# Where the last gate piece and the split of the next group stand in a gated-linear-attention kernel followed by a multiplicative feed-forward block

## The chip, the cores and the metric

The kernel runs on one core of one Trainium2 chip. The metric is the device time of one execution in microseconds. The kernel before took 459.05 us, the median of three runs (457.19, 459.05, 459.93).

## What is computed

For each of 4 batches and 8 heads a recurrence runs over 768 time steps, with heads of 48 values; its output, laid out as 3072 tokens by 384 values, goes through a feed-forward block with two multiplied factors:

```python
for t in range(S):
    state = alpha[:, :, t, :, None] * state + np.einsum('bhd,bhe->bhde', k[:, :, t], v[:, :, t])
    y[:, :, t] = np.einsum('bhd,bhde->bhe', q[:, :, t], state)
...
a = x @ w1        # (3072, 384) @ (384, 1024)
b = x @ w2
h = a * b @ w3    # (1024, 1024)
return (h @ w_out).astype(np.float32)   # (1024, 384)
```

The weights come as 64-bit floats and are converted on the chip from their bits.

## The kernel before

**Part 1, the attention.** The sequence is cut into N = 24 chunks of 128 tokens, six to a batch. The loop over n (0 to 24) is a pipeline written out by hand. A step n does, in the order of the program:

- attend_state(n - 1) (L473; L483 in early steps): the state T times q of the chunk before, into two banks of PSUM.
- scores(n) (L431): the products of keys and queries of chunk n, with some of the products of chunk n - 1 between them (attend_low, L420). VectorE masks the result (ms, L441; L458 in early steps).
- transposed(n + 1) (L383): TensorE transposes the scaled queries and keys of the next chunk, ScalarE copies them to qkT (L385).
- attend(n - 1) (L496): the rest of the products of masked scores and values; ScalarE copies them to x (L493, L498), and SP stores x to HBM (xd).
- outer(n) (L395): the outer products of keys and values; VectorE adds them to the state (L405). Nothing at the last chunk of a batch (n = 5, 11, 17, 23).
- decayed(n + 2) (VectorE, L361) scales queries and keys of chunk n + 2 into qk; logs(n + 4) (ScalarE L326 and L330, VectorE L331) takes logarithms of alpha; decays(n + 3) (TensorE L348) sums them, and ScalarE takes exponentials e of the sums (L351, L352).

**The gates.** While attention goes on, the two factors of the feed-forward block are computed for chunks that are done, in five early groups: four of 3 chunks and one of 4. The group's input is loaded from xd (load_early: into part of the tile x3b, for the last group into free input tiles). Then split_early cuts it into a high, a low and a middle part in 32-bit floats of reduced form: ScalarE makes the high part (L536), VectorE the low (L537) and the middle one (L539), which lies partly in tile x and partly in x3b. There is one such pair of tiles, so a split writes over what the gates of the group before read.

A gate is one tile of 128 of the 1024 columns: two pieces, one for each factor, each of 9 matmuls (L569) into two banks, six for the first and three for the second. ScalarE moves the first bank out (L578), VectorE adds the second (L580). After the second piece VectorE multiplies the two factors (L617), and the tile before this one is stored on SP's queue (L643). The first four groups do four tiles each in part 1, thus eight pieces a group. They wait in the list fill; run(pieces) takes some of them, at three places of a step: behind outer, behind logs and its conversions, and at the step's end behind decays.

**Conversions of weights** go on between: convert(steps) takes the next stage of a weight block (ScalarE L246, L251, L262; VectorE L247 to L267).

**Order.** Within an engine the instructions need not run in the order of the program; tc.issue_after (through after_marks) puts the instructions of a block behind a marked one on its own engine. Engines wait for each other through semaphores. PSUM has eight banks, all from one pool (bank). SP issues the loads and, in part 1, the stores.

Groups begin at steps 6 (FIRST), 9, 13, 17 and 21: begin has the keys 3, 7, 11, 15 and 19, and a group begins at n = key + 2 (group 0 at 6).

**Behind part 1** come the late gates with 512 columns, the product of w3 and w_out (fold), and the projection of all 24 chunks (project).

## Time and profile before

| what | value |
|---|---|
| median of 3 runs | 459.05 us (457.19 to 459.93) |
| the profiled execution's own time | 456.97 us |
| its span, first to last instruction | 455.2 us |
| TensorE matmuls busy | 442.2 us, 97% |
| TensorE weight loads busy | 392.9 us, 86% |
| VectorE / ScalarE / GpSimd busy | 369.8 / 279.3 / 85.5 us |
| granted TensorE clock | 0.999 |
| part 1 | to about 182 us |

The steps are found by the pair of copies to qkT (L385) that each has. Between the copies of one step and of the next one the engines are busy as follows; the four stretches that begin with a split's step are 75.18, 103.90, 132.50 and 160.75 (the windows view: from and to, length, then PE, PEld, DVE, ACT busy in us):

| stretch | length | PE | PEld | DVE | ACT | pieces in it |
|---|---|---|---|---|---|---|
| 75.18 to 81.62 (n = 9) | 6.44 | 4.82 | 4.24 | 5.66 | 6.03 | 0 |
| 81.62 to 89.38 | 7.76 | 7.76 | 7.32 | 7.67 | 5.53 | 3 |
| 97.43 to 103.90 (n = 12) | 6.47 | 6.47 | 6.03 | 6.36 | 5.82 | 2 |
| 103.90 to 109.19 (n = 13) | 5.29 | 5.10 | 4.42 | 5.25 | 5.24 | 0 |
| 125.56 to 132.50 (n = 16) | 6.94 | 6.94 | 6.50 | 4.49 | 5.28 | 2 |
| 132.50 to 137.28 (n = 17) | 4.78 | 4.67 | 3.98 | 4.25 | 4.72 | 0 |
| 153.80 to 160.75 (n = 20) | 6.95 | 6.95 | 6.50 | 5.53 | 4.03 | 2 |
| 160.75 to 165.03 (n = 21) | 4.28 | 4.19 | 3.87 | 3.87 | 4.22 | 0 |

In rows of the timeline stand: start, duration, engine, line, operation, what is written and read, count, and in brackets the idle time before it with what ended it. A row can merge several instructions. In rows of waits: who waited for whom, us in total, times, longest.

### The profile page before, as it was taken

Reading aid. Unit: us, or ns where it says so; the run is one execution under the profiler, and the core shown is the slowest. Engines: PE = TensorE matmul, PEld = TensorE weight load, DVE = VectorE, ACT = ScalarE, POOL = GpSimd, SP = SyncE. Lnnn points to the kernel's source line nnn. Section 1 sums busy time; section 2 is a strip of 40 time slices with the busy share of each in tenths; the row PEclk is TensorE's granted clock in tenths of the full one; section 3 lists DMA queues with packets and bytes.
Section 4 is the critical chain, followed back from the end, with each engine's and each line's share of the span. In section 5 each row is a group of like instructions: output and inputs, shape, how many; then the busy total and the mean of one; then the engine's idle time right before and its main releaser. Section 6 shows DMA issues by size and latency. Waiting matters only on the chain.

```text
span 455.2 us, 11107 instructions
## 1 busy us (share of the span) xinstructions
PE 442.2 (97%) x4304; PEld 392.9 (86%) x4304; DVE 369.8 (81%) x600; ACT 279.3 (61%) x523; POOL 85.5 (19%) x171
## 2 busy tenths in 40 slices
PE   4999998999999999999999999999999999999996
PEld 2677797998988988888888888888888999999996
DVE  2799997999979898899998999999427576776671
ACT  4698966779688673978875766575436333333430
POOL 6244341335225330021121010100010000000000
PEclk9999999999999999999999999999999999999999
DMA  9999999999888763466775263600129555565411
GB/s 205 246 263 235 256 248 232 229 228 236 211 185 208 198 176 106 148 184 176 251 231 184 95 187 114 208 32 38 48 89 279 175 176 165 168 192 171 151 51 52
DMA packets 149381, 79.98 MB, mean 176 GB/s; under 512 B 97184, under 2 KB 138784, under 8 KB 149328
## 3 DMA queue, kind: packets, MB, share of 16 engines
q1 hardware_dynamic: 143840, 64.84, 53.4%
q0 software_dynamic: 5488, 14.43, 10.1%
q8 instruction: 34, 0.56, 0.5%
q14 instruction: 19, 0.16, 0.1%
HBM read 57.19 MB, written 22.06 MB: 174 GB/s over the span
## 4 chain that ended last, share of the span: by engine, by line
PE 94%; ACT 2%; DVE 1%; issue 1%; DMA 1%; DVEq 0%; ACTq 0%
PE bank L569 74%; PE bank L383 3%; PE bank L342 2%; PE bank L431 2%; PE bank L455 2%; PE bank L473 2%; PE bank L502 2%; PE bank L395 2%; PE bank L496 1%; PE bank L348 1%; PE bank L345 1%; PE bank L420 1%; PE bank L483 1%; DMA ac<-in_alpha_dram 1%; ACT x L536 0%
## 5 line engine op out<-in xcount | busy, mean ns | idle before, releaser
L569 PE MATMUL bank<-x,w 128*128 128x512 f32 (+1 forms) x688 | 161.8, 373 | 0.7 <-ACT e L352 0.4
L569 PEld LDWEIGHTS bank<-x,w 128*128 128x128 f32 x688 | 124.7, 188 | 19.6 <-ACT e L352 0.7
L569 PE MATMUL bank<-w3o,ab 128*128 128x384 f32 x576 | 100.2, 335 | 0.0
L569 PEld LDWEIGHTS bank<-w3o,ab 128*128 128x128 f32 x576 | 99.9, 188 | 0.2
L569 PE MATMUL bank<-x3b,w 128*128 128x512 f32 (+1 forms) x248 | 71.6, 384 | 0.0
L594 ACT ACTIVATE bank<-bank 128x512 f32<-128x512 f32 (+1 forms) x72 | 41.1, 571 | 32.2 <-PE bank L569 32.2
L569 PEld LDWEIGHTS bank<-x3b,w 128*128 128x128 f32 x248 | 46.5, 188 | 8.2 <-issue 0.3
L643 POOL DMA_DIRECT2D abd<-r x33 | 19.3, 583 | 140.0 <-DVE r L629 117.4
L693 DVE TENSOR_TENSOR ab<-abl,ab 128x1024 fp32r<-128x1024 f32 x24 | 29.4, 1226 | 14.3 <-ACT ab L692 14.3
L385 ACT COPY qkT<-bank 128x512 f32<-128x512 f32 x48 | 25.9, 590 | 23.8 <-PE bank L383 23.8
L578 ACT ACTIVATE t<-bank 128x384 f32<-128x384 f32 x24 | 11.8, 493 | 46.0 <-PE bank L569 46.0
L692 ACT ACTIVATE ab<-abl 128x1024 fp32r<-128x1024 f32 x24 | 25.5, 1061 | 21.7 <-PE bank L569 19.8
L569 PE MATMUL bank<-wo,w3T 128*128 128x384 f32 x192 | 36.3, 337 | 0.0
L569 PEld LDWEIGHTS bank<-wo,w3T 128*128 128x128 f32 x192 | 34.1, 188 | 1.2
L580 DVE SCALAR_TENSOR_TENSOR o<-bank,t 128x384 f32<-128x384 f32 x24 | 13.4, 558 | 25.9 <-issue 14.3
L251 ACT ACTIVATE power<-power,rebias 128x512 uint32<-128x512 uint32 (+1 forms) x36 | 25.0, 695 | 13.1 <-DVE power L250 12.9
L629 DVE TENSOR_TENSOR r<-bank,r 128x512 f32<-128x512 f32 x32 | 21.8, 682 | 9.3 <-PE bank L569 8.6
L361 DVE TENSOR_TENSOR qk<-kq,e 128x768 f32<-128x768 f32 x24 | 23.0, 957 | 7.7 <-ACT e L352 7.7
L694 DVE SCALAR_TENSOR_TENSOR ab<-ab,abl 128x1024 fp32r<-128x1024 f32 x24 | 29.2, 1218 | 0.0
L580 DVE SCALAR_TENSOR_TENSOR r<-bank,r 128x384 f32<-128x384 f32 (+1 forms) x40 | 22.9, 578 | 6.5 <-ACT r L578 5.1
L253 DVE SCALAR_TENSOR_TENSOR mant<-mant,raw 128x512 f32<-128x512 uint32 (+1 forms) x36 | 23.5, 653 | 3.2 <-ACT raw L246 3.2
L578 ACT ACTIVATE r<-bank 128x384 f32<-128x384 f32 (+1 forms) x40 | 20.5, 515 | 8.6 <-PE bank L569 7.0
(119 smaller groups left out, 748.8 us busy)
## 6 DMA issues: line engine op xcount, KB each, us to landing
abl<-abd SPq DMA_DIRECT2D x24, 512.0 KB, 4.2
abd<-r POOLq DMA_DIRECT2D x33, 256.0 KB, 3.1
raw<-in_moe_w_dram SPq DMA_DIRECT2D x64, 128.0 KB, 3.9
raw<-in_moe_w_dram SPq DMA_DIRECT2D x12, 512.0 KB, 5.3
kq<-in_k_dram SPq DMA_DIRECT2D x24, 192.0 KB, 4.8
kq<-in_q_dram SPq DMA_DIRECT2D x24, 192.0 KB, 4.6
xd<-x SPq DMA_DIRECT2D x48, 96.0 KB, 3.4
xT<-xd POOLq DMA_DIRECT2D x6, 768.0 KB, 5.3
```

What stands on the lines that cost most here:

```text
L251: nc.scalar.activation(power, power, AF.Relu, scale=2.0 ** 23, bias=rebias)
L253: nc.vector.scalar_tensor_tensor(mant, top, 2.0 ** -20, rest, op0=ALU.mult, op1=ALU.add)
L361: mark["qk", n] = nc.vector.tensor_mul(qks[n % 3][:, :, :, 0:D], st.pop(("kq", n)), st.pop(("e", n)).rearrange("p i (h d) -> p i h d", h=H ...
L385: mark["qkT", n] = nc.scalar.copy(qkT[:, :, :, ds(DP * half, DP)], tp[half]).ins
L569: nc.tensor.matmul(p, w[part][i], x[part][i], start=start and part == parts[0] and i == 0, stop=stop and part == parts[-1] and i == n - 1, ...
L578: mark["scale"] = nc.scalar.activation(t, p1, AF.Copy, scale=(1.0 + 1.0 / P) * scale).ins
L580: nc.vector.scalar_tensor_tensor(to, p2, scale, t, op0=ALU.mult, op1=ALU.add)
L594: mark["scale"] = nc.scalar.activation(p, p, AF.Copy, scale=1.0 + 1.0 / P).ins
L629: nc.vector.tensor_mul(r[0], p, r[0])
L692: nc.scalar.activation(t[:, 0], ab, AF.Copy, scale=1.0 - 2.0 ** -13)
L693: nc.vector.tensor_sub(t[:, 1], ab, t[:, 0].bitcast(FP32))
L694: nc.vector.scalar_tensor_tensor(t[:, 2], t[:, 0].bitcast(FP32), -1.0 - 1.0 / P, ab, op0=ALU.mult, op1=ALU.add)
```

## The change

A group's eight pieces came in the steps behind its split as 3, 3, 2, 0; now they come as 3, 3, 1, 1, for group 0 (steps 7 to 9) as 4, 3, 1 in place of 5, 3, 0. The last of them stands in the next split's step behind outer(n), as the only piece there. The split stands behind that piece and behind decayed(n + 2), no longer behind transposed(n + 1). On its engines it is put behind the masks of chunk n, the copies to qkT of chunk n + 1, and, new, the scaled queries and keys of chunk n + 2. The conversion that followed the split (its VectorE instructions are marked behind x3, the split's last instruction) goes with it. The last group's pieces in part 1 (3, 3, 2 from step 22) stay.

```diff
-        if n - 2 in begin and n > FIRST:
-            g, tiles = begin[n - 2]
-            with after_marks(("ms", n), ("qkT", n + 1)):
-                split_early(g)
-            fill.extend(gate(g, f) for f in tiles)
+        next_group = n - 2 in begin and n > FIRST
...
-        pieces = ((3, 3, 2, 0) if n > FIRST + 3 else (0, 3, 3, 0))[(n - FIRST) % 4] if n >= FIRST else 0
+        pieces = 0 if n <= FIRST else (2, 3, 1)[n - FIRST - 1] if n < FIRST + 4 else (3, 3, 1, 1)[(n - FIRST) % 4] if n < N - 2 else (3, 3, 2)[n - N + 2]
...
-        marks = (*[("qkT", n + 1)] * (n < N - 1), *[("qk", n + 1), ("ms", n)] * early, *["x3"] * (n - 2 in begin and n > FIRST))
-        if n < N - 2 and n != FIRST:
+        marks = (*[("qkT", n + 1)] * (n < N - 1), *[("qk", n + 1), ("ms", n)] * early)
+        if n < N - 2 and n != FIRST and not next_group:
             with after_marks(*marks):
                 convert(2 if early else 1, raws)
...
         outer(n)
         if n > FIRST:
             third(ready)
-        run(pieces > 0)
+        if not next_group:
+            run(pieces > 0)
...
             decayed(n + 2)
+        if next_group:
+            run(pieces)
+            assert not fill
+            g, tiles = begin[n - 2]
+            with after_marks(("ms", n), ("qkT", n + 1), ("qk", n + 2)):
+                split_early(g)
+            fill.extend(gate(g, f) for f in tiles)
+            with after_marks("x3"):
+                convert(1, raws)
...
-        run(pieces > 1)
+        run(pieces > 1 and not next_group)
...
-        run(pieces > 2)
+        run(pieces > 2 and not next_group)
```

## The prediction, made before the change was run

> **What bounds the kernel.** I read the page's engine rows and chain first, then the waits of TensorE and of its weight loads in part 1, then part 1's timeline, engine by engine, and the DMA view of short stretches.
>
> ```profile
> PE 442.2 (97%) x4304; PEld 392.9 (86%) x4304; DVE 369.8 (81%) x600; ACT 279.3 (61%) x523; POOL 85.5 (19%) x171
> ...
> PE 94%; ACT 2%; DVE 1%; issue 1%; DMA 1%; DVEq 0%; ACTq 0%
> ```
>
> TensorE carries the chain to the end. The change leaves its work as it is, so it can only win where TensorE stands still in part 1, or make it stand still anew. PE busy hides small holes (ends are modelled), so I measure from start to start. An undisturbed step and the one after it, a split's step (n = 13):
>
> ```profile
> 100.06 1.55 PE L569 MATMUL bank<-x,w 128*128 128x384 f32 x8
> ...
> 101.62 0.51 PE L348 MATMUL bank<-la,sums 128*128 128x384 f32 x2
> ...
> 105.42 0.69 PE L473 MATMUL bank<-qkT,T 48*64 48x64 f32 x32
> 106.26 0.40 PE L431 MATMUL bank<-qkT 48*64 48x128 f32 x7
> ...
> 108.52 0.62 PE L395 MATMUL bank<-v,qk 128*64 128x48 f32 x16
> 109.36 1.62 PE L569 MATMUL bank<-x,w 128*128 128x384 f32 x7 [0.21 <-ACT e L352]
> ...
> 112.75 0.51 PE L348 MATMUL bank<-la,sums 128*128 128x384 f32 x2
> ```
>
> One gate piece (9 matmuls) takes 101.62 - 100.06 = 1.56 us, a step without pieces about 3.7. What is late behind the split: L473 takes 106.26 - 105.42 = 0.84 instead of 0.52 (114.75 to 115.27 in the next step), L395 takes 0.84 instead of 0.55, two pieces 3.39 instead of 3.23. Together 0.32 + 0.29 + 0.16 = 0.77 us. In the same way I get 1.31 around n = 17 (0.25, 0.29, 0.28, 0.06, 0.07, 0.36) and 0.74 around n = 21 (0.05, 0.16, 0.05, and 0.48 in the first three pieces, 6.85 against 6.37). Around n = 9 the hole is of another kind:
>
> ```profile
> 79.46 0.21 PE L420 MATMUL bank<-ms,vt 64*64 64x64 f32 x1 [1.62 <-issue]
> ```
>
> The row is of TensorE's timeline: nothing that the profile shows held it for 1.62 us (the weight loads 1.76). The DMA view from 77.0 to 79.0 has
>
> ```profile
> q8 instruction: 1, 0.02, 2.9%
> ```
>
> One packet of the instruction queue lies in the hole, while the data queue fills the engines (101% of their time); from 67.9 to 77.0 there is none, at 98%. By the packets' starts most other fetches of part 1 are 4 to 8 us apart. I read the hole as TensorE running out of instructions in the stretch with the most of them (158 matmuls in 6.45 us).
>
> All holes: 1.76 + 0.77 + 1.31 + 0.74 = 4.6 us. That is the most that the change can win.
>
> **What the change does.** Of each early group's eight pieces one leaves the step before the split's step (for group 0, step 7) and stands in the split's step, n = 9, 13, 17, 21, behind outer(n). The split, which stood ahead of attend(n-1), stands behind this piece.
>
> *Pieces.* TensorE: -1.56 and +1.56, zero in work, four times. The piece's eviction on ScalarE (L578, 0.50), on VectorE (L580, 0.55) and the product (L617, 0.56) move with it. The store of the previous tile (L643) moves a step too: on SP its data have long been there, so it holds nothing behind it; SP's waits in that step are for buffers. If it did block SP's 192 KB loads, cover is a step or more (loads are issued three to five steps ahead). Step 7 loses a piece while VectorE is full (11.04 of 11.07 us from 55.20), but step 8 leaves it idle before L580 (1.09, 0.40) and its own results are asked for a step later, so I take zero there, between 0 and +0.5.
>
> *Absolute times.* TensorE is 1.56 us earlier up to outer(13), then runs the piece, and ends it at 104.87, where it came to L348 before. The split must wait for the piece's last matmul, since it overwrites the tile x that the piece reads. Before, it began on ScalarE at 104.86 behind the copies of qkT. So it does not start later by a step but by a few tenths. What differs is what ScalarE and VectorE have already done by then.
>
> ```profile
> 104.86 1.18 ACT L536 ACTIVATE x<-x3b 128x1152 fp32r<-128x1152 f32 x1
> 105.93 0.63 ACT L262 ACTIVATE w<-mant 128x512 fp32r<-128x512 f32 x1
> ...
> 108.03 0.48 ACT L351 ACTIVATE e<-bank 128x384 f32<-128x384 f32 x1
> ```
>
> ScalarE has no idle time from 103.90 to past 109 (between these rows stand the copies of x, 106.57 to 107.71, and la): the exponentials of a bank that TensorE finished at 105.4 run at 108.03 to 109.3, and L569 waits for them at 109.36. After the change the copies of qkT (from about 102.35) and of x (to about 104.5) lie ahead of the split. Then L578 to 105.1, split to 106.3, exponentials to about 107.3 to 108.3: no wait is left.
>
> *The next group's first piece, n = 13.* It comes at 105.42 (behind L348, 0.44) + 0.52 + 1.04 (scores and transposed products) + 0.64 (transposes) + 0.52 (L496) + 0.55 (L395) = 108.6. The high part is done by 106.3. VectorE: L580 and L617 to about 106.3, then 1.35 for the low part (107.9), 1.26 and 0.55 for the rest (109.1, 109.7). TensorE asks for the low part 0.1 + 3 x 0.174 later (109.2), the rest from 109.7, its last third at 110.1. It fits, by 1.3, 0.6 and 0.4 us. Gain 0.8, between 0 (the exponentials still late) and 0.77.
>
> *n = 9.* The same, and 1.56 us of TensorE work between the request of instructions and their use. If the request follows TensorE's progress, the hole shrinks by about 1.5; if it only waits for the DMA engines to come free, not at all. I take 1.2: of 34 packets of that queue only this one has such a hole behind it once the inputs have come (from 30 us on), so something about this stretch makes it, and the stretch gets longer. Range 0 to 1.76.
>
> The Trainium skill, Runtime: NRT & Kernel Launch, section Instruction fetch mechanics, says that TensorE's instructions come in blocks of 16 KiB fetched by its own queue while the present block runs, and that this is mostly hidden. The row agrees on the block (0.02 MB) and not on the hiding. What hangs on the rule is rival D.
>
> *n = 17.* VectorE is full from 130.6 to 156, with two steps of weight conversion behind the split (L264, L267), and at 140.34 TensorE's loads wait for masks (L441, 0.34). VectorE's split started at 134.67 and starts at about 134.8 now; from there its row is the same. So what ScalarE gives back ahead of 140.34 (0.5) is mostly waited out there. I take 0.2, between -0.1 and 0.8.
>
> *n = 21.* The split comes in three parts and TensorE waits at 166.5 for the last low part:
>
> ```profile
> 162.60 0.96 DVE L537 TENSOR_TENSOR x<-kq,x 128x768 fp32r<-128x768 f32 x1 [0.36 <-ACT x L536]
> ```
>
> In the waits of the queue of weight loads this is
>
> ```profile
> PEld bank L569 <- DVE x L537: 0.6, 1, 0.6
> ```
>
> Now L580 and L617 of the piece (ending about 162.9, as its matmuls end at 161.7) stand before this instruction, so it starts 0.3 later, and with it TensorE. It ends with -0.3 to 0.3; I take a loss of 0.2.
>
> **Sum.** 1.2 + 0.8 + 0.2 - 0.2 = 2.0 us earlier at the end of part 1. From 180 us on TensorE's rows show no wait, so it is kept to the end. The profiled execution took 456.97 us (span 455.2 and 1.8 around it): 455.0. The median of the runs shown, 459.05, lies 2.1 above it; I forecast 459.05 - 2.0 = 457.0.
>
> **Rivals.** *A, more holes than the profile shows (chance 0.17).* The three runs spread over 2.7 us and the profiled one lies below them. If what they have more is waiting for instructions in the other dense stretches (n = 17 and 21, fetches at 132.56 and 159.47 with little time before their use), the extra work there covers it too: 2.0 + about 2.1 = 4.1, 454.9. For: the DMA share is 0.86 to 1.07 in every step up to 125 us. Against: the profile has one such hole.
>
> *B, nothing is won (0.16).* The fetch is late for the DMA's sake, so n = 9 keeps its hole, and ScalarE puts la or w ahead of the exponentials, so n = 13 waits as before: 0 + 0 + 0.2 - 0.2 = 0, 459.05. That the change does not do what it says is part of it: order on an engine isn't the program's (qk of n = 15 runs on VectorE at 103.61, ahead of the masks of n = 13, though written behind them).
>
> *C, the split becomes late (0.17).* The order on VectorE decides: if the four masks of the next step (0.74 + 0.86 = 1.6 us) run ahead of the split, its end goes from 109.7 to 111.3. The last third was asked for at 110.1, so TensorE waits from a delay of 0.4 us on. Against its place before (109.52 + 1.5 = 111.0 with the old waits), that is 0.3 to 1.2 lost, according to how far the low part waits too. I price the groups at 1.0 and n = 21, which has no slack, at 1.9: 4.9 lost, less the 1.2 of n = 9: 459.05 + 3.7 = 462.8. For: the slack is tenths. Against: the masks need scores that end at about 106.9, when the split could be running.
>
> *D, the hole at n = 9 is an accident of the one execution (0.10).* Then other executions of the kernel before have nothing there to win back, and the sum is 0.8 + 0.2 - 0.2 = 0.8: 458.25. For: 33 of 34 fetches leave no such hole. Against: it lies just where TensorE works off the most instructions. The section named above speaks for D.
>
> **Chances.** Forecast 0.40, A 0.17, B 0.16, C 0.17, D 0.10. A measurement of this kernel tells some 0.5% (2.3 us) from no change. The forecast's terms run from about 0 to 3.3 us, so 0.20 of its 0.40 lies beyond 2.3; with A, faster is 0.37. Same: 0.20 + 0.16 + 0.10 = 0.46. Slower: 0.17. The range goes from A (453.9, with all 4.6 and some tenths) to 461.5, which leaves out most of C. The likeliest case by itself: 455.7 to 459.1.
>
> **What would show it.** Right: in the split's steps L473 and L395 back at 0.52 and 0.55; ScalarE idle before the split; the first two pieces behind it in 3.23; no 1.6 us without a releaser; VectorE's split starting within 0.5 us of the same place. Wrong: LDWEIGHTS L569 waiting for x of L537 or L539 in steps 10, 14 or 18 (C); an issue wait still there (B); masks on VectorE between the two parts of a split (C).

## The result and the profile after

The kernel after takes 459.26 us (median of 20 runs, 458.11 to 460.69), the kernel before in the same comparison 457.19 (20 runs, 454.84 to 460.62). The ratio is 1.0044, with a 95% interval of 1.0025 to 1.0063: 2 us slower, where 2 us faster was forecast. It is under the 0.5% that the prediction called no change, but clear of 1. That 459.26 lies inside the forecast range (453.9 to 461.5) is luck: the range was counted from 459.05, and the kernel before took 457.19 here. The profiled execution has a span of 457.3 us, 2.1 more than before, at the same clock (0.999).

The page's engine rows and the summary of its chain:

```profile
PE 442.6 (97%) x4304; PEld 391.6 (86%) x4304; DVE 368.5 (81%) x600; ACT 278.6 (61%) x523; POOL 84.7 (19%) x171
...
PE 69%; DVE 3%; ACT 2%; DMA 1%; issue 1%; SPq 0%; DVEq 0%; ACTq 0%
```

The work is the same, and TensorE still leads the chain. The two chain rows can't be compared as they stand: after the change the chain is followed back only to 110.88 us, so its shares add up to 76%, of which TensorE has 69. To see where the time went, I measure from the start of one chunk's transposes (L383) to the next; those of chunk n + 1 lie in step n, so the stretch from chunk n + 1 to n + 2 holds what stands behind outer(n) and the scores of the next step. The moved piece (1.57) is taken off where it lies inside. Gains against the profiled execution of before, in us:

| group | forecast | split's own stretch | steps behind it | together |
|---|---|---|---|---|
| up to chunk 10, equal work | 0 to -0.5 | | | -0.91 |
| n = 9 (10 to 11, then to 13) | +1.2 | +1.89 | -1.53 | +0.36 |
| n = 13 (14 to 15, then to 16) | +0.8 | +0.38 | -1.29 | -0.91 |
| n = 17 (18 to 19, then to 21) | +0.2 | +0.31 | -0.77 | -0.46 |
| n = 21 (22 to 23, then to the end) | -0.2 | -0.09 | -0.07 | -0.16 |

The sum is -2.1. The split's own stretches win 2.5 us, even more than forecast; the steps behind them lose 3.7. Against a second profile of the kernel before (b_again, below) the same five rows are -1.09, +0.10, -0.76, -1.03 and -0.05, in sum -2.8: the loss stays, its shares among the groups don't. TensorE's timeline of n = 13, first the split's step, then the first two pieces behind it:

```profile
105.97 0.69 PE L473 MATMUL bank<-qkT,T 48*64 48x64 f32 x32
106.49 0.39 PE L431 MATMUL bank<-qkT 48*64 48x128 f32 x8
...
108.69 0.62 PE L395 MATMUL bank<-v,qk 128*64 128x48 f32 x16
109.24 1.61 PE L569 MATMUL bank<-x,w 128*128 128x384 f32 x6
111.03 0.58 PE L569 MATMUL bank<-x,w 128*128 128x384 f32 x2 [0.17 <-DVE x L539]
111.44 0.41 PE L569 MATMUL bank<-x3b,w 128*128 128x384 f32 x1
112.53 1.68 PE L569 MATMUL bank<-x,w 128*128 128x384 f32 x8 [0.68 <-DVE ms L441]
...
114.22 0.51 PE L348 MATMUL bank<-la,sums 128*128 128x384 f32 x2
```

L473 takes 0.52 and L395 0.55, as in an undisturbed step. But the two pieces take 114.22 - 109.24 = 4.98 us, against 3.39 before. ScalarE and VectorE at that place:

```profile
105.93 0.50 ACT L578 ACTIVATE r<-bank 128x384 f32<-128x384 f32 x1
106.32 1.17 ACT L536 ACTIVATE x<-x3b 128x1152 fp32r<-128x1152 f32 x1
```

```profile
103.50 0.74 DVE L441 TENSOR_TENSOR ms<-bank,keep 64x256 int32<-64x256 int32 x2
...
105.06 0.95 DVE L361 TENSOR_TENSOR qk<-kq,e 128x768 f32<-128x768 f32 x1
105.92 0.35 DVE L405 TENSOR_TENSOR tmp<-bank,T 128x192 f32<-128x192 f32 x1
106.19 0.68 DVE L264 SCALAR_TENSOR_TENSOR w<-w,mant 128x512 fp32r<-128x512 f32 x1
106.79 0.69 DVE L267 SCALAR_TENSOR_TENSOR w<-w,mant 128x512 fp32r<-128x512 f32 x1
107.39 0.55 DVE L580 SCALAR_TENSOR_TENSOR r<-bank,r 128x384 f32<-128x384 f32 x1
107.86 0.42 DVE L247 TENSOR_SCALAR mant<-raw 128x512 uint32<-128x512 uint32 x1
108.20 0.55 DVE L617 TENSOR_TENSOR r<-r 128x384 f32<-128x384 f32 x1
108.67 1.35 DVE L537 TENSOR_TENSOR x<-x3b,x 128x1152 fp32r<-128x1152 f32 x1
...
111.74 0.74 DVE L441 TENSOR_TENSOR ms<-bank,keep 64x256 int32<-64x256 int32 x2
```

The split's low part begins at 108.67 on VectorE, where it began at 106.29. Ahead of it stand the piece's L580 and L617, as forecast, and three conversions (L264, L267, L247) that nobody had reckoned with; before, they ran behind it. The masks of chunk 14 (L441) stand behind the split. A gate uses nothing that they write; what it waits for is the PSUM bank with the scores that they read. The second profile of the kernel before (b_again) has on VectorE:

```profile
105.78 0.35 DVE L405 TENSOR_TENSOR tmp<-bank,T 128x192 f32<-128x192 f32 x1
106.05 1.35 DVE L537 TENSOR_TENSOR x<-x3b,x 128x1152 fp32r<-128x1152 f32 x1
...
109.44 0.74 DVE L441 TENSOR_TENSOR ms<-bank,keep 64x256 int32<-64x256 int32 x2
```

From 103 to 118 VectorE is busy 14.84 of 15.00 us after the change and 14.85 in that second profile: what runs first delays all that follows. The waits of the queue of weight loads from 50 to 180 us show what followed (us in total, times, longest):

```profile
PEld bank L569 <- ACT qkT L385: 1.7, 2, 1.3
PEld bank L569 <- PE bank L569: 1.6, 2, 1.2
PEld bank L569 <- DVE x L537: 1.4, 2, 1.0
...
PEld bank L569 <- DVE ms L441: 1.3, 2, 0.9
```

Of the 1.4 for x (L537), 0.35 is in step 14 and 1.0 in step 22, where the kernel before waited 0.6; the 1.3 for masks is 0.9 in step 14 and 0.4 in step 18.

In step 10 it is a chain: VectorE's split ends at 81.17, then come L247 and L250, ScalarE's L251 waits for L250, the copies of qkT of chunk 11 stand behind L251, and TensorE waits for their bank:

```profile
81.88 0.72 ACT L251 ACTIVATE power<-power,rebias 128x512 uint32<-128x512 uint32 x1 [1.93 <-DVE power L250]
82.51 1.06 ACT L385 COPY qkT<-bank 128x512 f32<-128x512 f32 x2
```

```profile
83.12 0.30 PEld L569 LDWEIGHTS bank<-x,w 128*128 128x128 f32 x2 [1.27 <-ACT qkT L385]
```

In step 19 the order of two VectorE groups is turned round: qk (L361) is now ahead of the masks of chunk 19, and TensorE's matmuls wait 0.87 for the masks at 149.25 (the row of the weight loads names TensorE's own bank, 1.17).

```profile
149.25 0.59 PE L569 MATMUL bank<-x,w 128*128 128x384 f32 x2 [0.87 <-DVE ms L441]
```

```profile
147.35 1.10 DVE L361 TENSOR_TENSOR qk<-kq,e 128x768 f32<-128x768 f32 x1
148.37 0.74 DVE L441 TENSOR_TENSOR ms<-bank,keep 64x256 int32<-64x256 int32 x2
```

In the second profile of the kernel before:

```profile
145.61 0.74 DVE L441 TENSOR_TENSOR ms<-bank,keep 64x256 int32<-64x256 int32 x2
...
147.16 0.95 DVE L361 TENSOR_TENSOR qk<-kq,e 128x768 f32<-128x768 f32 x1
```

At n = 21 the low part starts at 165.08 in place of 162.60. The order of VectorE's instructions is set when the program is built, by an ordering that moves unmarked instructions forward. Written in letters (M masks, S s s the split's low and middle parts, E L580, P L617, Q qk, c a conversion, T the state, l L331), from the masks of chunk n on:

```
n = 13   before  M T S s s l M c c T E Q      after  M Q T c c E c P S s s l M T Q E
n = 17   before  M S s s c c l M T Q E E      after  M E P S s s c c l M T Q E c E
n = 19   before  M Q T c c E   (Q behind M)   after  Q M T c c E   (Q ahead of M)
```

### The profile page after: what moved, and what is told of

Its sections match the earlier page's. It is cut to its first block, busy times and chain, and to the rows that moved or that the text cites. A ratio compares the mean times of both kernels' runs of the same rounds, so it can differ in the third digit from the quotient of the medians.

```text
span 457.3 us, 11126 instructions
## 1 busy us (share of the span) xinstructions
PE 442.6 (97%) x4304; PEld 391.6 (86%) x4304; DVE 368.5 (81%) x600; ACT 278.6 (61%) x523; POOL 84.7 (19%) x171
## 4 chain that ended last, share of the span: by engine, by line
PE 69%; DVE 3%; ACT 2%; DMA 1%; issue 1%; SPq 0%; DVEq 0%; ACTq 0%
PE bank L569 65%; PE bank L473 1%; DMA v<-in_v_dram 1%; PE bank L431 1%; PE bank L496 1%; DVE ms L441 1%; PE bank L383 1%; DVE x3b L539 0%; PE bank L420 0%; DVE qk L361 0%; DMA xd<-x 0%; ACT x L493 0%; PE bank L348 0%; ACT x L536 0%; PE bank L395 0%
## 5 line engine op out<-in xcount | busy, mean ns | idle before, releaser
L569 PE MATMUL bank<-x,w 128*128 128x512 f32 (+1 forms) x688 | 163.1, 374 | 3.5 <-DVE ms L441 1.6
L569 PEld LDWEIGHTS bank<-x,w 128*128 128x128 f32 x688 | 124.1, 188 | 24.1 <-ACT qkT L385 1.7
L569 PE MATMUL bank<-w3o,ab 128*128 128x384 f32 x576 | 100.2, 334 | 0.0
L569 PEld LDWEIGHTS bank<-w3o,ab 128*128 128x128 f32 x576 | 99.9, 188 | 0.2
L569 PE MATMUL bank<-x3b,w 128*128 128x512 f32 (+1 forms) x248 | 71.5, 384 | 0.0
L569 PEld LDWEIGHTS bank<-x3b,w 128*128 128x128 f32 x248 | 46.4, 188 | 8.2 <-issue 0.2
L578 ACT ACTIVATE t<-bank 128x384 f32<-128x384 f32 x24 | 11.8, 493 | 45.8 <-PE bank L569 45.8
L569 PE MATMUL bank<-wo,w3T 128*128 128x384 f32 x192 | 36.3, 337 | 0.0
L569 PEld LDWEIGHTS bank<-wo,w3T 128*128 128x128 f32 x192 | 34.1, 188 | 1.2
L251 ACT ACTIVATE power<-power,rebias 128x512 uint32<-128x512 uint32 (+1 forms) x36 | 25.1, 696 | 15.5 <-DVE power L250 15.5
L580 DVE SCALAR_TENSOR_TENSOR o<-bank,t 128x384 f32<-128x384 f32 x24 | 13.4, 558 | 26.0 <-issue 14.3
L580 DVE SCALAR_TENSOR_TENSOR r<-bank,r 128x384 f32<-128x384 f32 (+1 forms) x40 | 22.8, 578 | 10.4 <-ACT r L578 9.0
L361 DVE TENSOR_TENSOR qk<-kq,e 128x768 f32<-128x768 f32 x24 | 23.3, 970 | 8.2 <-ACT e L352 7.5
L253 DVE SCALAR_TENSOR_TENSOR mant<-mant,raw 128x512 f32<-128x512 uint32 (+1 forms) x36 | 23.6, 655 | 3.1 <-ACT raw L246 3.1
L578 ACT ACTIVATE r<-bank 128x384 f32<-128x384 f32 (+1 forms) x40 | 20.4, 514 | 9.1 <-PE bank L569 8.9
```

The lines of the kernel that those rows point to most:

```text
L251: nc.scalar.activation(power, power, AF.Relu, scale=2.0 ** 23, bias=rebias)
L253: nc.vector.scalar_tensor_tensor(mant, top, 2.0 ** -20, rest, op0=ALU.mult, op1=ALU.add)
L361: mark["qk", n] = nc.vector.tensor_mul(qks[n % 3][:, :, :, 0:D], st.pop(("kq", n)), st.pop(("e", n)).rearrange("p i (h d) -> p i h d", h=H ...
L569: nc.tensor.matmul(p, w[part][i], x[part][i], start=start and part == parts[0] and i == 0, stop=stop and part == parts[-1] and i == n - 1, ...
L578: mark["scale"] = nc.scalar.activation(t, p1, AF.Copy, scale=(1.0 + 1.0 / P) * scale).ins
L580: nc.vector.scalar_tensor_tensor(to, p2, scale, t, op0=ALU.mult, op1=ALU.add)
```

## The experiments

Theory 1 at first: the moved piece holds the split up. Its rival: the split's new place, and the order on VectorE that comes of it. Theory 2, beside it: group 0's pieces in the full step 7 and 8. Later the first was replaced by: VectorE's order and load behind a split make the masks late, and with them a bank. "10 to 23" is from the transposes of chunk 10 to those of chunk 23, without the moved piece: 88.94 in the profiled execution before, 90.07 after. Each variant has one profile, the kernels before and after have two each; where a kernel has two, they agree within 0.3 over this stretch. The start up to chunk 9 differs by up to 4 us from execution to execution (63.8 to 68.1 over all profiles, with 1.57 added where the moved piece of group 0 is missing before it), so the times of variants that lie within 0.3% of each other are not told apart. The ratios are those on record, each to runs of the kernel before beside the variant (medians there from 457.19 to 458.38); at this size they can differ from the quotient of two medians (e_conv_behind: 458.58 over 457.35 is 1.0027, on record 0.9990).

**b_again**: the kernel before, profiled a second time.

> The kernel before, unchanged, once more with a profile. If the hole of 1.62 us at n = 9 (TensorE without a releaser) belongs to that stretch, it stands here again, of 1 to 2 us, at the second half of scores(10). If it is an accident of one execution, there is none there, perhaps one elsewhere, and the kernel after won nothing by losing it.

456.23 us; 10 to 23 takes 88.72. The hole of 1.76 us at n = 9 is not there, so rival D was right about this execution. But the steps without it are hardly shorter: 10 to 11 takes 4.12 in place of 5.70, 11 to 12 takes 9.48 in place of 8.51, as waits for qkT and for exponentials come up that the hole had covered. The hole is not worth 1.76.

**e_split_only**: the change with the pieces as before, so that the split's place alone is changed.

```diff
-        pieces = 0 if n <= FIRST else (2, 3, 1)[n - FIRST - 1] if n < FIRST + 4 else (3, 3, 1, 1)[(n - FIRST) % 4] if n < N - 2 else (3, 3, 2)[n - N + 2]
+        pieces = ((3, 3, 2, 0) if n > FIRST + 3 else (0, 3, 3, 0))[(n - FIRST) % 4] if n >= FIRST else 0
```

> Pieces as before (3, 3, 2, 0), only the split stands at its new place, behind decayed(n + 2). Theory 1 (the split ends late because the moved piece holds it: its matmuls, then its eviction and product on VectorE stand ahead): the kernel is as fast as before, within 0.7 us. Rival (the place itself is late: conversions of weights get ahead of the split on VectorE, its queue is in another order): it loses 1.5 to 3 us against before, with waits of L569 for L537 or for masks in steps 10, 14 and 18.

460.10 us, ratio 1.0041 (1.0008 to 1.0073); 10 to 23 takes 91.12. With no piece ahead of it the split is as dear as the whole change, so theory 1 is not supported, though the lower end of the interval (0.4 us) still lies within the 0.7 that it allowed. At n = 13 two conversions stand ahead of the low part:

```profile
105.72 0.68 DVE L267 SCALAR_TENSOR_TENSOR w<-w,mant 128x512 fp32r<-128x512 f32 x1
106.44 0.62 DVE L247 TENSOR_SCALAR mant<-raw 128x512 uint32<-128x512 uint32 x1
106.97 1.35 DVE L537 TENSOR_TENSOR x<-x3b,x 128x1152 fp32r<-128x1152 f32 x1
```

**e_piece_first**: the piece and the split both at the split's old place, ahead of attend(n - 1).

```diff
+            run(pieces)
+            assert not fill
+            pieces = 0
             g, tiles = begin[n - 2]
             with after_marks(("ms", n), ("qkT", n + 1)):
                 split_early(g)
```

> Pieces as in the changed kernel (3, 3, 1, 1), but in the split's step the piece stands at the split's old place, ahead of attend(n - 1) and outer(n), and the split right behind it. The split gets the 1.07 us of attend and outer as extra time before its readers. Theory 1: the waits behind the split (1.75 at n = 14, 1.26 at n = 10) shrink by about 1 each, the kernel is 2 to 3 us faster than the changed one, at or below before. Rival (it is the place of the split and the order on VectorE, or the early steps): 0 to 1 us faster than the changed one.

459.38 us, 1.0018 (0.9988 to 1.0049); 10 to 23 takes 90.82. Inconclusive in time; in the trace the stretch is no shorter than after the change.

**e_group0_old**: the change, but group 0 with its pieces in the old steps.

```diff
-        pieces = 0 if n <= FIRST else (2, 3, 1)[n - FIRST - 1] if n < FIRST + 4 else (3, 3, 1, 1)[(n - FIRST) % 4] if n < N - 2 else (3, 3, 2)[n - N + 2]
+        pieces = 0 if n <= FIRST else (3, 3, 0)[n - FIRST - 1] if n < FIRST + 4 else (3, 3, 1, 1)[(n - FIRST) % 4] if n < N - 2 else (3, 3, 2)[n - N + 2]
```

> As the changed kernel, but group 0's pieces come as before (5, 3, 0 in steps 7 to 9); groups 1 to 3 as changed. Theory 2 (with a piece less, step 7 gets ahead of the weights' loads: ScalarE stands at L246 until a load lands, with L578 and the exponentials behind it, 0.85 us of TensorE at the transposes of step 8 and 0.47 at the pieces behind): 1.0 to 1.4 us faster than the changed kernel there, so about 0.7 us slower than before, less what n = 9 loses without its piece. Rival (the waits in steps 7 and 8 come from late inputs of that one execution): as slow as the changed kernel, 2 us over before.

460.80 us, 1.0060 (1.0026 to 1.0095); 10 to 23 takes 91.00. From chunk 9 to 10 it takes 9.09, near the 8.91 of before and not the 10.23 of after, but 8 to 9 takes 14.81 where before took 12.68: ScalarE waits 3.20 for raw weights (L246) there, one stretch earlier than in the kernel after (2.42). The loss moved with that wait, and theory 2 is not supported.

**e_hold**: the change, and conversions of the two steps behind a split marked to stay behind it.

```diff
-        marks = (*[("qkT", n + 1)] * (n < N - 1), *[("qk", n + 1), ("ms", n)] * early)
+        marks = (*[("qkT", n + 1)] * (n < N - 1), *[("qk", n + 1), ("ms", n)] * early, *["x3"] * (n > FIRST + 3 and (n - 3 in begin or n - 4 in begin)))
```

> As the changed kernel, but the conversions of weights of the two steps behind a split (L264, L267 and L247, L250 at n = 13) are marked behind the split on VectorE, where they ran ahead of it (1.72 us at n = 13). Theory 3 (what is late behind the split is VectorE's row as a whole: everything that gets ahead of the split there shifts the split, the next masks and so the banks): VectorE's split at n = 13 starts at most 0.6 us behind the transposes of step 14 instead of 1.13 behind them, the first two pieces of step 14 take 3.3 to 3.9 us instead of 4.98, from the transposes of step 9 to those of step 23 about 1 us less than in the changed kernel (100.3 after taking off the moved piece). Rival (only the matmuls of the moved piece hold the split): no change there, split as late as before.

458.09 us, 1.0014 (0.9982 to 1.0045); 10 to 23 takes 90.07. At n = 13 the split begins 0.02 ahead of the transposes of chunk 15, where it began 1.13 behind them, as expected; but the two pieces still take 4.74. The wait has moved: the second bank of the first piece now comes last (0.92), again released by masks. Here the theory took its final form.

**e_conv_behind**: e_hold, and no conversion in the split's step; the next step does it.

```diff
-            with after_marks("x3"):
-                convert(1, raws)
...
+                convert(2 if early or n - 3 in begin and n > FIRST + 1 else 1, raws)
```

> As the run before it, and the split's own step (n = 9, 13, 17) converts nothing: its conversion steps come in the next step, behind the copies to qkT. Theory 3 with ScalarE's part: at n = 10 L251 no longer stands ahead of the copies to qkT (ScalarE idle 1.93 us there, TensorE 1.27 behind it); the first two pieces of step 10 take 3.2 to 3.6 us instead of 4.5, in all 1.5 to 2.5 us less than the changed kernel from step 9 to step 23, about as fast as before. Rival (conversions come back as waits a step later): the sum stays at that of the changed kernel.

458.58 us, 0.9990 (0.9959 to 1.0021); 10 to 23 takes 92.16, with a hole for instructions in step 9. Time and trace point in opposite ways; inconclusive.

**e_evict_behind**: the change, with the moved piece's L580 and L617 behind the split on VectorE.

```diff
+        if between:
+            between()
+        with after_marks(*["x3"] * bool(between)):
+            nc.vector.scalar_tensor_tensor(to, p2, scale, t, op0=ALU.mult, op1=ALU.add)
...
+            def between():
+                with after_marks(("ms", n), ("qkT", n + 1), ("qk", n + 2)):
+                    split_early(g)
```

> As the changed kernel, but on VectorE the eviction and the product of the moved piece (L580, L617, about 1.1 us) stand behind the split instead of ahead of it. Theory 3: the split starts earlier where ScalarE's part is done before them: at n = 21 by 0.3 to 1.0 us, and the wait of the first pieces there (7.22 us for three against 6.37) shrinks by as much; at n = 9 and 17 by 0.1 or less, at n = 13 by up to 1. In all 0.5 to 1.5 us less than the changed kernel. Rival (the bank that L580 holds longer is missed): waits of L348 or L473 for L580, no gain.

460.85 us, 1.0080 (1.0055 to 1.0106); 10 to 23 takes 92.52. The split is earlier (at n = 13, 0.63 behind the transposes of chunk 15 in place of 1.13), and it costs more: the bank that this eviction (L584 in this kernel) frees is missed at once. The loads' waits:

```profile
PEld bank L569 <- DVE r L584: 4.2, 5, 1.8
```

**e_before_free**: the kernel before, its split without marks.

```diff
-            with after_marks(("ms", n), ("qkT", n + 1)):
-                split_early(g)
+            split_early(g)
```

> The kernel before, with no mark on the split: it may run as soon as the last piece of the step before is done, ahead of the masks and of the copies to qkT. Theory 3, other direction (an earlier split is worth what a later one costs): VectorE's split starts 2 us or more ahead of the transposes of step n + 1 where it stood 1.1 to 1.2 ahead, no waits for x, and from step 9 to step 23 0.5 to 1.5 us less than before. Rival (VectorE is full in these steps, so any order only moves the wait): masks or qk late instead, attend or transposes wait, as slow as before or slower.

467.88 us, 1.0209 (1.0158 to 1.0261). Too early is worse than too late: masks and qk stand behind the split. TensorE's waits from 50 to 180 us:

```profile
PE bank L383 <- DVE qk L361: 4.8, 3, 1.8
PE bank L473 <- DVE ms L441: 3.1, 4, 1.1
```

**e_decayed_behind**: the change, with qk behind the masks in steps 11, 15, 19 and 23. The condition of the edit also holds at n = 7, and so the mark stands there too, in the variants below that use it as well.

```diff
-        with after_marks(*[("ms", n)] * (n <= FIRST)):
+        with after_marks(*[("ms", n)] * (n <= FIRST or n - 4 in begin)):
             decayed(n + 2)
```

> The kernel after, with decayed(n + 2) of the steps 11, 15, 19 and 23 put behind the masks of chunk n on VectorE. In the kernel after the scaled queries and keys (L361, 1.10) run ahead of the masks of chunk 19 (L441 at 148.37), in the second look at the kernel before behind them; TensorE's second bank of the first piece waits for these masks (0.9 to 1.2), and the stretch from the transposes of chunk 20 to those of chunk 21 takes 9.64 against 8.55. Theory: the order on VectorE costs that. Then this stretch takes 8.5 to 8.7 here, the stage from the transposes of chunk 9 to those of chunk 23 about 99.2 in place of 100.3, and the kernel is about 1 us faster than the kernel after (ratio to before about 1.002). Rival: VectorE is full, so whatever runs first makes something else late; the stretch stays above 9.3 and the ratio at 1.004.

459.78 us, 1.0040 (1.0007 to 1.0073). 20 to 21 takes 9.05, between the two expectations, and 10 to 23 is 89.67. But the conversions around n = 13 moved too, and the split there is later (1.45 behind the transposes of chunk 15).

**e_order**: both marks.

> The last one, and also the marks that keep conversions of the two steps behind a split behind it. Theory (order on VectorE): 20 to 21 at 8.5 to 8.7, and the split of n = 13 at most 0.1 behind the transposes of chunk 15 in place of 1.13; the wait in step 14 stays, since the evictions of the moved piece (1.1 us) still stand ahead of the split; stage about 99.0, ratio to before 1.001 to 1.003. Rival (VectorE full): stage 100.0 to 100.3, ratio 1.003 or more.

458.34 us, 1.0027 (1.0003 to 1.0051); 10 to 23 takes 89.24, 0.8 less than after the change and 0.3 to 0.5 more than before. 20 to 21 stays at 9.65, against the expectation, with another wait in step 19, now for L580 (0.84). At n = 13 VectorE has the piece and the split without conversions between:

```profile
106.16 0.56 DVE L580 SCALAR_TENSOR_TENSOR r<-bank,r 128x384 f32<-128x384 f32 x1 [0.19 <-ACT r L578]
106.76 0.56 DVE L617 TENSOR_TENSOR r<-r 128x384 f32<-128x384 f32 x1
107.23 1.35 DVE L537 TENSOR_TENSOR x<-x3b,x 128x1152 fp32r<-128x1152 f32 x1
...
110.31 0.74 DVE L441 TENSOR_TENSOR ms<-bank,keep 64x256 int32<-64x256 int32 x2
```

and the bank is free when these two masks end, 110.31 + 0.74 = 111.05. TensorE's matmuls at the same place:

```profile
108.95 1.31 PE L569 MATMUL bank<-x,w 128*128 128x384 f32 x6
111.20 0.59 PE L569 MATMUL bank<-x,w 128*128 128x384 f32 x2 [0.93 <-DVE ms L441]
```

**b_order**: the kernel before with the same two marks.

> The kernel before with the two marks of the last comparison: conversions of the two steps behind a split stay behind it, and decayed(n + 2) of the steps 11, 15, 19, 23 behind the masks. The kernel after gained 1.9 us in its stage by them (100.3 to 98.4, against 97.6 and 97.9 of before). Theory (the change upset the order on VectorE; the order of before was already good): here they gain next to nothing, stage 97.3 to 97.9, ratio 0.999 to 1.001. Rival (the marks help every kernel, and the change costs its 2 us on top of any order): stage about 96, ratio 0.996 or less.

458.22 us, 1.0038 (1.0009 to 1.0068); 10 to 23 takes 89.20. The marks give the kernel before nothing, so they do not help every kernel. The ratio lies outside what was expected, and its trace doesn't explain it (span 455.3, before 455.2): a ratio of 1.004 by itself does not show that a stretch of part 1 got longer, and this holds for the change's own 1.0044 too.

**e_product_behind**: e_order, with L617 of the moved piece behind the split; L580 stays ahead.

> The kernel after with both marks, and the product (L617, 0.55) of the moved piece behind the split on VectorE; its eviction (L580) stays ahead, so that the bank comes free as early as before. Theory: what is still lost with the order mended (0.6 us in the stage) comes from 1.03 us of the moved piece's work on VectorE ahead of the split; with half of it gone, the split begins 0.5 us earlier against the transposes (n = 13: -0.5 in place of -0.01), the wait in step 14 shrinks from 1.2 to 0.7, the stage is 98.0, and the ratio to before 0.999 to 1.002. Rival: the next wait behind it (the low part, the masks, a later bank) takes its place; stage 98.3 or more, as without this edit.

457.83 us, 1.0006 (0.9985 to 1.0027), but 10 to 23 takes 90.50. The time came out as the theory said, the mechanism did not: at n = 13 the split begins at the same place (-0.02), since VectorE now waits for the high part.

```profile
105.92 0.56 DVE L580 SCALAR_TENSOR_TENSOR r<-bank,r 128x384 f32<-128x384 f32 x1 [0.19 <-ACT r L578]
106.97 1.46 DVE L537 TENSOR_TENSOR x<-x3b,x 128x1152 fp32r<-128x1152 f32 x1 [0.49 <-ACT x L536]
```

The high part (L536, 105.78 in this kernel) stands on ScalarE behind the copies of x and behind L578. Clearing VectorE alone does not bring the split forward.

**b_gpsimd, a_gpsimd**: the kernels before and after with the product of an early gate on GpSimd.

```diff
-        nc.vector.tensor_mul(r[0], *r)
+        nc.gpsimd.tensor_mul(r[0], *r)
```

> The kernel before, with the product of the two factors of an early gate (L617, 0.55 us on VectorE, 20 times) on GpSimd. By GpSimd's row for 128x192 (0.72 us) one product there takes an estimated 1.3 us; GpSimd is busy about 6 of 18 us in these stretches. Theory (VectorE has too much to do behind a split): less waits, the stage from transposes 9 to 23 goes from 97.7 to about 97, 0.5 to 1 us faster than before (ratio 0.998 to 0.999). Rival: GpSimd's copies for the turned values (L167) or the stores come late, or GpSimd and VectorE slow each other; same or slower, with waits of TensorE for POOL vt.

> The kernel after, with the product on GpSimd. Theory: with 0.55 us less on VectorE between the moved piece and the split, and 1.6 us less in a step with three pieces, the masks of the next chunks come in time more often: the split of n = 13 begins 0.5 us earlier, and the kernel loses less against the kernel before with the same edit than the 2 us between the kernels without it: 0 to 1 us. Rival: what the change loses does not come from VectorE; the difference stays at 2 us.

461.84 us, 1.0114 (1.0081 to 1.0148), and 467.53 us, 1.0217 (1.0191 to 1.0243). The rival for the kernel before was right; of the two expectations for their difference neither came out, as it grew to 5.7 us. The product takes 1.1 us there:

```profile
L617 POOL TENSOR_TENSOR r<-r 128x384 f32<-128x384 f32 x16 | 17.7, 1107 | 19.8 <-DVE r L580 13.1 <-issue 4.6 <-PE bank L348 1.9
```

and VectorE did not come free, because other instructions of it became longer (last section). That a less loaded VectorE lets the change win was therefore not tried by this.

**a_again**: the kernel after, profiled a second time.

> The kernel after, unchanged, a second look. From the transposes of chunk 9 to those of 10 the first look has 10.23, every look at the kernel before 8.91. If that is the change (group 0's pieces later, step 8 full), it is 10 or more again; if it is one execution's late weights, 8.9 to 9.2. From the transposes of chunk 10 to those of chunk 23 the first look has 91.64, that is 90.07 without the piece that lies inside; theory (order on VectorE, which is fixed in the program): 89.6 to 90.6 again, against 88.7 to 89.2 of the kernel before. Rival (the loss is of one execution): within 0.3 of before.

459.15 us, span 457.4. 9 to 10 takes 10.41, 10 to 23 takes 90.29, and single stretches agree with the first profile within 0.3. The loss from 10 to 23 is the program's; the one from 9 to 10 has late weights beside it in both profiles ("Step 7 at zero", below).

**e_conv_order, b_conv_order**: e_order, and the kernel before, with both marks and no conversions in the steps 9, 13 and 17.

> The kernel after with both marks, and no conversion in the step of a split (n = 9, 13, 17); it is made in the next step behind the masks. Theory (VectorE's order and load behind a split): the masks of the step behind each split come right behind it; ratio to before 0.997 to 1.001, better than with the marks alone (1.0027). Rival: the conversions fill the next step instead and move the wait there; ratio as with the marks alone or more.

> The kernel before with the same three edits. If the edits pay in any kernel, it is at or below 0.997; if they only mend what the change upset, it is 0.999 to 1.002; if the next step's conversions delay it, above. Its difference to the run above is what the change alone gives when the order is the same: the forecast's own terms would have the kernel with the change 2 us (0.4 per cent) faster; what the runs up to now show lets expect 0 +- 0.3 per cent.

458.24 us, 1.0008 (0.9981 to 1.0036), and 457.09 us, 1.0005 (0.9974 to 1.0035). With the change 10 to 23 takes 88.64, the shortest of all kernels with it and like before (88.72 to 88.94), although TensorE still waits for masks, 0.66 in step 14; the same edits in the kernel before leave its time as it was, while its one profile takes 91.84 from 10 to 23, with the hole of the prediction again, longer. The means of the twelve runs of each differ by 0.4 us (458.3 with the change, 458.0 without), with an estimated interval of 1.3 either way from their spread. So with the order mended neither the gain of 2 us nor the loss of 2 us is left; smaller ones are not excluded. The hole in b_conv_order:

```profile
79.70 0.13 PEld L420 LDWEIGHTS bank<-ms,vt 64*64 64x64 f32 x1 [2.59 <-issue]
```

No kernel here beats the kernel before by more than its interval.

## Why the prediction was wrong

**Right.** TensorE carries the chain; the clock is the same. In the splits' steps L473 and L395 are back at 0.52 and 0.55, no 1.6 us without a releaser is left in either profile of the kernel after (though the second profile of before has none either), and the exponentials no longer hold L569. The own stretches won 2.5 us against the first profile of before and 2.0 against the second, where 2.0 was forecast for all. Of the steps' other work nothing else moved: from chunk 23 to the end it is 291.93 against 291.86.

**The step that failed: "Absolute times".** It said that the split starts later by a few tenths, and named 0.5 us as the bound. On VectorE it starts 1.1, 2.4, 1.5 and 2.5 us later (78.48, 108.67, 136.15, 165.08 against 77.35, 106.29, 134.67, 162.60). At n = 13 the parts are:

- TensorE was 1.0 us earlier there, not 1.56 (transposes of chunk 14 at 102.15 against 103.16), by the loss up to chunk 10, less what n = 9 won.
- The high part on ScalarE begins at 106.32, not 105.1: behind the exponentials, la and a conversion (L262) the copies of qkT begin at 103.78, not 102.35; the copies of x end at about 106.0, and only then comes L578. ScalarE has no idle time ahead of the split; such idle time was named as a sign of being right. With its 1.17 the high part ends at 107.5.
- On VectorE three conversions, 0.68 + 0.69 + 0.42, run ahead of the split. The prediction took "L580 and L617 to about 106.3, then 1.35" and held the order for given. It knew that this order isn't the program's (it says so under rival B), and its sum has no term for it; rival C prices one such order, masks ahead of the split, at a chance of 0.17.

Two sums in "The next group's first piece" are loose: the terms behind 105.42 give 108.7, not 108.6, and 106.3 + 1.35 is 107.65, not 107.9. Beside 2.4 us neither matters.

**The next group's first piece.** The sum reckoned with what the piece reads: high, low and middle part. It left out where it writes. The bank that TensorE asks for is released by the masks of the next chunk, which follow the split on VectorE; even with the low part in time (e_order) the piece waits 0.93 for them. Rival C came nearest: the order on VectorE decides, and the split becomes late. Its sign, weight loads of L569 waiting for x of L537, is there in step 14 (0.35). But it has masks only as work that delays the split, and what ran ahead were conversions. Its price, 1.0 for a group, was near what n = 13 lost (0.91), not n = 17 (0.46) or n = 9; its place, the low part, is the smaller wait in step 14 (0.35, against 0.94 for the masks).

**n = 9, 1.2.** The hole is not what its length says. After it the next stretch is 1.0 shorter, in the kernel before (5.70 + 8.51 = 14.21 against 4.12 + 9.48 = 13.60) and in kernels with the change (e_order, with a hole of 0.87: 6.38 + 8.77 = 15.15; after, without: 5.38 + 9.76 = 15.14). So by these pairs the term should have been 0 to 0.6. The longest hole is not made up in this way: b_conv_order, with 2.59, takes 6.53 + 10.02 = 16.55, against 13.61 in b_order without a hole; but its conversions stand in other steps, so this is no clean pair. Nor does the piece cover the hole: e_order, e_conv_behind and e_conv_order have the piece and a hole of 0.9 to 1.0. Rival D was the better reading: at this place the hole comes in some executions (0.6 to 2.6 us in 8 of 19 profiles), with and without the change. That it is a wait for instructions, as the prediction read it, fits all eight: TensorE goes on 1.3 to 1.5 us after the end of the packet of 16384 bytes on the instruction queue that lies before it. This packet starts 1.2 to 3.6 us behind the transposes of chunk 10 there, and 0.9 to 1.6 (once 2.7) in the eleven others. The Trainium skill, Runtime: NRT & Kernel Launch, section Instruction fetch mechanics, calls the fetches mostly hidden; at this one 11 profiles agree and 8 don't.

**n = 17 and 21.** VectorE's split at n = 17 was to start at 134.8 and starts at 136.15; two steps later qk stands ahead of the masks (1.1 us, in step 19), which no part of the sum had. At n = 21 the forecast of a small loss came out (-0.2; -0.16 by the table) by luck: the low part was to start 0.3 later, and with it TensorE; it starts 2.5 later, the wait for it grows from 0.57 to 1.01, and the rest of these steps makes that up.

**Step 7 at zero.** 0.8 to 1.1 is lost up to chunk 10 in both profiles of the kernel after. There ScalarE waits 2.4 to 2.6 for raw weights (L246), L578 stands behind it, and the transposes of chunk 9 wait 0.7 to 0.9 for that bank:

```profile
63.30 0.66 ACT L246 ACTIVATE raw<-raw 128x512 f32<-128x512 uint32 x1 [2.42 <-DMA raw<-in_moe_w_dram]
```

Of the eleven profiles with this piece moved, six have this wait (1.8 to 2.6) and take 9.86 to 10.41 from chunk 9 to 10; five don't have it there and take 8.91 to 9.19, nearly as before (8.91). So the loss goes with late weights and does not come in every execution; with the pieces moved and the weights in time, zero was about right. None of the six profiles with the old split and the old pieces has such a wait, and both with the new split and group 0's old pieces have one (2.25 and 3.20); whether the change makes the weights late more often stays open.

**What is shown and what isn't.** That the order on VectorE was upset, and that undoing it by marks takes 0.8 us (e_order) and with fewer conversions 1.4 to 1.6 us (e_conv_order) from 10 to 23, one trace of each shows. The other three kernels with the split's new place and the conversions held behind it don't show it there: e_hold 90.07, e_product_behind 90.50, e_conv_behind 92.16, against 90.07 and 90.29 after the change. In times it is shown only for kernels together: the five with the split's new place and the conversions held behind it have a mean ratio of 1.0009 (1.0014, 0.9990, 1.0027, 1.0006, 1.0008), the change 1.0044, the split's place alone 1.0041. Single steps between these are smaller than their intervals. That the order is the whole of the loss is therefore argued, not shown.

## What to carry to other kernels

A wait taken out of one step is won only if the engines that come next have room: follow the split, the masks behind it and the bank that they free, not only the operand. Where the order on an engine is made by an ordering that moves instructions forward, a moved block changes that order steps away; compare the order of each engine before pricing the move. And a hole's length is its worth only if nothing else comes late behind it: take the length of the two steps, with and without.

## What the runs showed of the hardware

GpSimd's work lengthens VectorE's, by the kind of operand and mostly where the two meet. With the product on GpSimd (b_gpsimd), between 50 and 180 us:

```profile
L361 DVE TENSOR_TENSOR qk<-kq,e 128x768 f32<-128x768 f32 x16 | 18.0, 1127 | 0.9 <-ACT e L352 0.6
L580 DVE SCALAR_TENSOR_TENSOR r<-bank,r 128x384 f32<-128x384 f32 x32 | 17.0, 550 | 6.5 <-ACT r L578 6.5
L331 DVE TENSOR_TENSOR la<-la,la 128x384 fp32r<-128x384 f32 x14 | 10.2, 732 | 0.7 <-ACT la L330 0.6
...
L254 DVE SCALAR_TENSOR_TENSOR power<-raw,power 128x512 uint32<-128x512 uint32 x6 | 6.0, 1007 | 0.0
L537 DVE TENSOR_TENSOR x<-x3b,x 128x1152 fp32r<-128x1152 f32 x4 | 5.7, 1431 | 0.8 <-ACT x L536 0.7
```

In the second profile of the kernel before the means are 963, 550, 549, 730 and 1417 ns. Five groups with two operands in SBUF became 17 to 38% longer (L361, L331, L254, and L264 and L267 with 681 to 904 and 682 to 812); others with two such operands (L537, L539, L253, L255) hardly changed. The difference is whether an instruction runs at the same time as a product on GpSimd: of the 16 of L361 the five that do take 1.46 us in the mean and the other eleven 0.98, and of the 14 of L331 nine take 0.82 and five 0.58; no L537 or L539 of these groups does. L267 is an exception: none of its six does, and it became longer all the same. L580, which reads one operand from PSUM, takes 0.55 either way, and the masks (L441) don't change either. In a_gpsimd three of the four L537 run at the same time as a product, and take 2.05 where the fourth takes 1.36: the split itself became longer, at the place where the change is already late. The Trainium skill, SBUF — State Buffer, section SBUF: two separate sides, says that a VectorE instruction with two SBUF inputs and a GpSimd one that reads SBUF exclude each other for a whole instruction; these times agree. In b_gpsimd the five groups take 9.0 us more, about the 9.2 that the 16 products had taken on VectorE.
